# Seven products for the first pass's down projection, with its activations kept in DRAM

## The chip, the cores and the metric

The kernel runs on one core of one Trainium2 chip. The metric is the device time of one execution in microseconds. Three runs of the kernel before gave a median of 1057.07 us (1052.88 to 1057.88).

## What is computed

Attention of 4 batches x 12 heads x 448 tokens x 64, with a soft cap, is followed by two layers on the 1792 x 768 result (d_ff is 2048). The second layer has no part in the edit, but is in the kernel:

```python
scores = cap * tanh(q @ k.T / sqrt(64) / cap)
x = softmax(scores) @ v            # heads side by side: 1792 x 768
h = x @ moe_w_in                   # 768 x 2048
g = h - tanh(h)
x = g @ moe_w_out                  # 2048 x 768
h = x @ moe2_w_in
g = h * sigmoid(1.702 * h)
out = g @ moe2_w_out
```

The four weight matrices come as float64.

## The kernel before

**Tiling.** Activations lie transposed, 128 features on the partitions and tokens along the free axis. The tokens are worked through in two passes, the first of 768 and the second of 1024 (`TOKENS`). A matmul has 128 x 128 weights and takes half a pass, 384 or 512 columns. Each factor is split into a high part (rounded to fp32r) and a low part (the rest); a product is three matmuls: high x high, high x low, low x high. A split is one cast on ScalarE (`hi_act`, L81) and one subtraction on VectorE (`lo_dve`, L93).

**Stages.** After attention (to 187.8 us) come, in this order: **P1-up** (`gemm_in(0)`, first pass, 16 blocks f of 128 features, 36 matmuls each); **P1-down** (`gemm_out`, L927); **P2-up** (`gemm_in(0)` again, second pass); **P2-down** (`gemm_out_seven`, L979); **P2-gate** (`gemm_in_seven`, the second layer's up projection of the second pass); then `gemm_rows_seven`, and both stages of the second layer for the first pass. "Seven" means that a product of 2 x 2 blocks is done by seven half-size products instead of eight: each sums blocks of weights (made once, kept in DRAM as `s1` to `s4`, `t1` to `t4`) and blocks of activations (made just before use, in `right` and `left`), splits them, and adds the results. In P2-down each of the seven products has four steps; a step takes one weight block of 128 x 768 and issues 18 matmuls, and at each step `right` makes the next product's activations into a `ring` of eight split blocks. P1-down is the plain form: 2 halves x 8 steps x 36 matmuls, with g of all 16 blocks held split (`gh`, `gl`) in on-chip memory.

**Weights.** A block of float64 weights is loaded (`dbl_dma`, 768 KB), turned into float32 in three instructions (`conv_exp` and `conv_low` on ScalarE or VectorE, `conv_or` on VectorE, L219) and loaded again next to it. For w_in1 the split parts are kept in DRAM for the second pass (`kept`). w_out1 is converted and split for P1-down at the time of use, and its float32 blocks are written to DRAM (`single`), read back by `sums_a` during P2-up, summed, and stored. `sums_i` converts and sums moe2's w_in, `sums_b` its w_out. In the stages by seven products a block comes back by `fetch` into two or three buffers (`whole`, `spare`) and is split into `wh` and `wl`.

**Order.** Matmuls go in program order. Two blocks of weights are prepared ahead (`LEAD`). Side work (`sums_a`, `sums_i`, `sums_b`) is cut into pieces by `yield`; `ahead` and `beside` add `rate[0]` to an account at each call and take a piece for each whole unit. Each piece stands behind the last instruction of ScalarE and VectorE in the trace at that point, with lower priority. All engines and SP's queue, which issues nearly all transfers, take their instructions in order. In an up projection, `g_cubic` takes tanh from PSUM, and a later call (`late`) does the rest: three ScalarE passes and three of VectorE over a block.

```python
    def g_split(f, g):
        yield hi_act(gh[f], g)
        yield lo_dve(gl[f], g, gh[f])
```

## Time and profile before

| | |
|---|---|
| median of three runs | 1057.07 us |
| profiled execution | 1055.68 us |
| its span | 1053.9 us |
| TensorE busy | 1038.7 us, 99% of the span, 5483 matmuls recorded |
| weight loads busy | 857.8 us, 81% |
| VectorE busy | 819.6 us, 78%, 1097 instructions |
| ScalarE busy | 692.0 us, 66% |
| granted clock of TensorE | 1.00 in all stages |
| transfers | 218.17 MB, mean 207 GB/s |

Shares over the whole span mix stages with different limits. The table says that TensorE is the engine to look at; whether another engine limits it in a stage shows in the view of busy time by stage, in the chain that ended last, and in the waits. Matmuls overlap, so the cost of one is read from the start of the first to the start after the last, not from the duration of one.

### The profile page before, as it was taken

To read this page: it belongs to the slowest core of one execution; us is meant where nothing else is said; L and a number is where in the kernel's file an instruction comes from. 1 tells how busy PE (TensorE), PEld (TensorE's weight loads), DVE (VectorE), ACT (ScalarE), POOL (GpSimd) and SP (SyncE) were. 2 spreads that over 40 slices of the span, in tenths; PEclk is the share of its full clock that TensorE was granted. 3 is DMA by queue.
4 is the path that set the end of the run, shared out by engine and by line. 5 is a ranking of instruction groups with operands and counts; after the bars stand their busy time and mean duration, and the time that the engine had idled before them with its cause. 6 is when DMAs were issued, how large, how long until landed. Compare 5 with 4: busy or idle time off the path is not lost.

```text
span 1053.9 us, 15397 instructions
## 1 busy us (share of the span) xinstructions
PE 1038.7 (99%) x5483; PEld 857.8 (81%) x5483; DVE 819.6 (78%) x1097; ACT 692.0 (66%) x958; POOL 56.1 (5%) x56
## 2 busy tenths in 40 slices
PE   8999999999999999999999999999999999999998
PEld 3333333899999998888878888887899999999998
DVE  4799999899986517988899897685899974448973
ACT  6999898787854335556775757655755745557663
POOL 0123444100000000000000000000000000000000
PEclk9999999999999999999999999999999999999999
DMA  5777688765588958888673852898654554444443
GB/s 132 196 217 219 181 228 257 255 228 192 195 257 275 327 170 287 289 277 283 219 253 118 299 183 82 272 321 297 224 164 126 190 155 130 129 118 143 153 134 104
DMA packets 153749, 218.17 MB, mean 207 GB/s; under 512 B 58380, under 2 KB 101704, under 8 KB 153672
## 3 DMA queue, kind: packets, MB, share of 16 engines
q1 hardware_dynamic: 152376, 216.58, 64.9%
q8 instruction: 43, 0.70, 0.3%
q10 hardware_dynamic: 1296, 0.61, 0.2%
...
## 4 chain that ended last, share of the span: by engine, by line
PE 81%; DVE 11%; ACT 3%; DMA 3%; issue 2%; SPq 0%; DVEq 0%; ACTq 0%
PE ps_o L1194 19%; PE ps_h L912 19%; PE ps_h L1092 19%; PE ps_y L952 9%; PE ps_y L1005 5%; PE ps_pv L568 3%; PE ps_sc L526 3%; DVE gr L361 1%; DVE wl L93 1%; ACT t L545 1%; DVE rl L93 1%; DVE ts L557 1%; PE ps_r L582 1%; DVE ts L556 1%; PE ps_tl L536 1%
## 5 line engine op out<-in xcount | busy, mean ns | idle before, releaser
L81 ACT CAST rh<-gr 128x512 fp32r<-128x512 f32 (+1 forms) x179 | 103.6, 584 | 99.7 <-PE ps_o L1194 63.2
L912 PE MATMUL ps_h<-x,wh 128*128 128x384 f32 (+1 forms) x672 | 153.0, 358 | 0.0
L93 DVE TENSOR_TENSOR rl<-gr,rh 128x512 fp32r<-128x512 f32 (+1 forms) x179 | 113.8, 642 | 25.8 <-ACT rh L81 25.1
L1194 PE MATMUL ps_o<-wh,rl 128*128 128x384 f32 x392 | 131.1, 334 | 0.0
L1194 PE MATMUL ps_o<-wh,rh 128*128 128x384 f32 x392 | 131.1, 334 | 0.0
L1194 PE MATMUL ps_o<-wl,rh 128*128 128x384 f32 x392 | 131.1, 334 | 0.0
L912 PEld LDWEIGHTS ps_h<-x,wh 128*128 128x128 f32 x672 | 121.1, 188 | 12.0 <-issue 0.7
L93 DVE TENSOR_TENSOR wl<-whole,wh 128x768 fp32r<-128x768 f32 (+1 forms) x103 | 94.0, 912 | 13.7 <-ACT wh L81 12.8
L81 ACT CAST wh<-whole 128x768 fp32r<-128x768 f32 (+1 forms) x103 | 82.4, 800 | 24.7 <-PE ps_h L1092 10.6
L1092 PE MATMUL ps_h<-x,wh 128*128 128x384 f32 (+1 forms) x336 | 97.3, 359 | 0.0
L912 PE MATMUL ps_h<-x,wl 128*128 128x384 f32 (+1 forms) x384 | 88.1, 364 | 0.0
L545 ACT ACTIVATE t<-ps_sc,tsc 128x896 f32<-128x896 f32 x72 | 69.8, 1005 | 15.1 <-PE ps_sc L526 15.0
L912 PEld LDWEIGHTS ps_h<-x,wl 128*128 128x128 f32 x384 | 69.8, 188 | 9.7 <-issue 1.4
L1194 PEld LDWEIGHTS ps_o<-wl,rh 128*128 128x128 f32 x392 | 73.6, 188 | 0.0
L1194 PEld LDWEIGHTS ps_o<-wh,rh 128*128 128x128 f32 x392 | 73.6, 188 | 0.0
L1194 PEld LDWEIGHTS ps_o<-wh,rl 128*128 128x128 f32 x392 | 73.6, 188 | 0.0
L547 ACT ACTIVATE t<-t,cpos 128x896 f32<-128x896 f32 x72 | 72.4, 1042 | 0.4
L526 PE MATMUL ps_sc<-qk 64*128 64x448 f32 x288 | 68.3, 568 | 2.3 <-ACT t L545 1.5
L361 DVE TENSOR_TENSOR gr<-gr 128x512 f32<-128x512 f32 (+2 forms) x112 | 69.3, 645 | 0.6 <-DMA gr<-xa 0.4
L361 DVE TENSOR_TENSOR part<-ps_h,part 128x512 f32<-128x512 f32 (+1 forms) x48 | 29.8, 621 | 51.3 <-PE ps_h L1092 51.1
L1092 PE MATMUL ps_h<-x,wl 128*128 128x512 f32 (+1 forms) x192 | 69.6, 362 | 0.0
L219 DVE SCALAR_TENSOR_TENSOR wr<-wr,wd 128x768 uint32<-128x768 uint32 x48 | 46.0, 961 | 28.4 <-ACT wd L211 20.7
...
## 6 DMA issues: line engine op xcount, KB each, us to landing
...
```

Of the source, the lines that this page charges most:

```text
L81: pin(nc.scalar.copy(out=dst, in_=src))
L93: return pin(nc.vector.tensor_tensor(out=dst, in0=src, in1=hi.bitcast(F32), op=ALU.subtract))
L219: pin(nc.vector.scalar_tensor_tensor(out=u, in0=u, scalar=3, in1=dbls.pop(i)[:, :, 0], op0=ALU.logical_shift_left, op1=ALU.bitwise_or))
L361: nc.vector.tensor_tensor(out=out, in0=a, in1=b, op=kind)
L526: pin(nc.tensor.matmul(ps[:, j, :S], qk[a, kc], qk[a, :S], start=True, stop=True))
L545: pin(nc.scalar.activation(out=t, in_=ps[:, :, :S], func=AF.Tanh, scale=tsc))
L547: ins = pin(nc.scalar.activation(out=tt[g, c], in_=tt[g, c], func=AF.Exp, scale=cpos))
L912: pin(nc.tensor.matmul(ps, w[:, kk, :], x[kk][:, a], start=(m == 0), stop=(m == len(seq) - 1)))
L952: nc.tensor.matmul(bank[e][:, :a1 - a0], w[:, kk, c], x[2 * j + kk][:, a0:a1], start=(j == 0 and m == 0), stop=(j == KF // 2 - 1 and m == ...
L1005: nc.tensor.matmul(ps[e], w[:, kk, c], x, start=(name == head and k == 0 and m == 0), stop=(k == KH - 1 and m == 2), skip_group_check=True,)
L1092: nc.tensor.matmul(ps, w, x, start=(name == head and m == 0), stop=(m == len(seq) - 1), skip_group_check=True,)
L1194: nc.tensor.matmul(ps[n], x[:, t], w[:, kk, :], start=(first and k == 0 and m == 0), stop=(k == KH - 1 and m == 2), skip_group_check=True,)
```

## The change

The order of the stages becomes P1-up, P2-up, P1-down, P2-down, and P1-down is done by seven products (`gemm_out_first`): the first pass's g leaves for DRAM after P1-up (`ga`), and comes back in 16 loads of a quarter of a block row each (`load_quarter`) into the room that the second pass's x had. The second pass's x is loaded and scaled in P1-up instead of P1-down. The products' activation sums are made in `first_right`; those of the first product are split during P2-up. w_out1 is no longer split from the converted block: `sums_a` converts it in groups of four blocks during P2-up and sums these in place, and P1-down fetches float32 blocks and sums as P2-down does. `sums_i` starts after `sums_a` and runs on through P1-down (rate 0.5 in its last six steps) and P2-down (1.1 instead of 0.8); `sums_b` runs at 1.45 instead of 1.2. The third buffer for weights is taken for every third block by number.

```diff
+    ga = dr_p.tile([2 * KM + 4, P, TOKENS[0]], F32, name="ga")
...
-    order = early + [i for i in range(R0) if i not in early] + [R0 + n % 4 * KQ + n // 4 for n in range(KF)]
+    order = early + [i for i in range(A0) if i not in early]
+    order += [A0 + n * KQ + j for j in range(KQ) for n in (3, 2, 0, 1)] + list(range(I0, R0)) + [R0 + n % 4 * KQ + n // 4 for n in range(KF)]
...
-    limit = [I0]
+    gr, wd_slot = [], []
+
+    limit = [A0]
...
+        elif A0 <= i < I0:
+            raws[i] = group[(i - A0) // KQ]
...
+    SEVEN_1 = ("11", "12", "s4", "s3", "s2", "s1", "22")
...
+            whole[i] = third[0] if third and i % 3 == 0 else wr_p.tile([P, WC], F32, tag="wr", name="whole")
...
     def sums_a():
+        limit[0] = I0
+        for _ in range(3):
+            dbl_dma()
+        yield
         for j in range(KQ):
-            r = four_of_pairs()
-            for n, t in enumerate(r):
-                nc.sync.dma_start(out=t, in_=single[n * KQ + j])
-                if n % 2:
-                    yield
-            for m, t in first_sums(*r):
+            group_of_four()
+            for n in (3, 2, 0, 1):
+                i = A0 + n * KQ + j
+                convert(i)
+                raws.pop(i)
+                yield
+            for m, t in first_sums(*group):
                 nc.sync.dma_start(out=side_a[m][j], in_=t)
                 yield
         done.add("a")
 
-    def sums_i(first, end):
-        limit[0] = I0 + 2 * end if end < KH else NCH
-        for _ in range(2):
...
-    def g_split(f, g):
-        yield hi_act(gh[f], g)
-        yield lo_dve(gl[f], g, gh[f])
...
+            q = gr[f][:, :n] if now[0] else first_g[f]
...
+            if not now[0]:
+                nc.sync.dma_start(out=ga[f], in_=q)
...
+        if now[0] and f < KH // 2:
+            for k in (2 * f, 2 * f + 1):
+                late.append(lambda k=k: split([t[:, :FH] for t in ring[k]], first_g[k][:, :FH]))
...
+    def open_first_g():
+        p = x_pool("ga")
+        for name in ("21", "22", "12", "11"):
+            quarter[name] = [p.tile([P, 2, FH], F32, name=f"g{name}_{n}") for n in range(KQ)]
...
+    def load_quarter(name, n):
+        f = 2 * n + (KH if name[0] == "2" else 0)
+        a = slice(FH, FT) if name[1] == "2" else slice(0, FH)
+        nc.sync.dma_start(out=quarter[name][n], in_=ga[f:f + 2, :, a].rearrange("k p c -> p k c"))
...
+    def first_right(p, k):
+        g11, g12, g21, g22 = (g_of(name, k) for name in ("11", "12", "21", "22"))
+        if p > 2:
+            with tc.issue_after(behind[k].ins):
+                if p == 3:
+                    sub(g12, g22, g12)
+                elif p == 4:
+                    add(g11, g11, ALU.add, g12)
+                elif p == 5:
+                    sub(g22, g22, g11)
+                elif p == 6:
+                    sub(g21, g21, g11)
+        behind[k] = split([t[:, :FH] for t in ring[k]], {1: g21, 2: g22, 3: g12, 4: g11, 5: g22, 6: g21}[p])
...
+                    if m == LATE_AT and a0 and not now[0]:
+                        if f:
+                            if loaded:
+                                x_scale(*loaded.pop(0))
+                        for _ in range(1 if f else 3):
+                            if todo:
+                                loaded.append((*todo[0], *x_load(*todo.pop(0))))
...
-    def gemm_out():
...
+    def gemm_out_first():
+        LO, HI = slice(0, FH), slice(FH, FT)
+        loads = [(name, n) for name in ("21", "22", "12", "11") for n in range(4)]
+        p1 = u3 = None
+        u7 = [g_of("12", e) for e in range(3)]
+        u1 = [g_of("12", 3 + e) for e in range(3)]
+        of, head_of = {}, {"s2": "11", "s1": "11", "22": "s3"}
+        step = 0
+
+        def leave(e, a, x):
+            nc.sync.dma_start(out=xa[e][:, a], in_=x)
+
+        six = [one_bank("ps_y")[:, :FH] for _ in range(6)]
+        nc.vector.memset(six[0][:1, :1], 0.0)
+        of["11"], of["12"] = six[1:4], six[4:] + six[:1]
+        for p, name in enumerate(SEVEN_1):
+            head = head_of.get(name, name)
+            if head not in of:
+                spread = [ps_s.tile([P, 512], F32, tag="s", name="ps_y") for _ in range(2 if head == "s4" else 0)]
+                of[head] = [t[:, :FH] for t in spread + [one_bank("ps_y") for _ in range(3 - len(spread))]]
+            ps = of[head]
+            for j in range(KQ):
                 i, (wh, wl) = w_next()
-                for (a0, a1), bank in zip(SPANS[0], ps):
-                    for e in range(3):
-                        c = slice(e * P, (e + 1) * P)
-                        seq = [p for kk in range(2) for p in ((wh, gh, kk), (wh, gl, kk))]
-                        seq += [(wl, gh, kk) for kk in range(2)]
-                        for m, (w, x, kk) in enumerate(seq):
+                for _ in range(2 if step < 2 else 1):
+                    if loads:
+                        load_quarter(*loads.pop(0))
+                rate[0] = .5 if step >= 22 else 0.0
+                ahead(i)
+                for e in range(3):
+                    c = slice(e * P, (e + 1) * P)
+                    for kk in range(2):
+                        k = 2 * j + kk
+                        h, l = (t[:, :FH] for t in ring[k])
+                        for m, (w, x) in enumerate(((wh, h), (wh, l), (wl, h))):
                             nc.tensor.matmul(
-                                bank[e][:, :a1 - a0], w[:, kk, c], x[2 * j + kk][:, a0:a1],
-                                start=(j == 0 and m == 0), stop=(j == KF // 2 - 1 and m == len(seq) - 1),
+                                ps[e], w[:, kk, c], x,
+                                start=(name == head and k == 0 and m == 0), stop=(k == KH - 1 and m == 2), skip_group_check=True,
                             )
+                if 1 <= step <= KQ:
+                    for k in (2 * step - 2, 2 * step - 1):
+                        first_right(1, k)
+                if p:
+                    for k in (2 * j, 2 * j + 1):
+                        if p < 6:
+                            first_right(p + 1, k)
+                        else:
+                            right(0, k)
+                if step == 0:
+                    run_late()
+                step += 1
+            if p == 0:
+                p1 = [part_of(t) for t in ("far", "far", "v")]
+            elif p == 2:
+                u3 = [part_of(t) for t in ("q", "q", "t")]
+            with tc.high_priority(offset=AHEAD):
+                for e in range(3):
+                    if name in ("11", "s4", "s3", "s2"):
+                        nc.scalar.copy(out={"11": p1, "s4": u3, "s3": u7, "s2": u1}[name][e], in_=ps[e])
+                    elif name == "12":
+                        add(p1[e], ps[e], ALU.add, p1[e])
+                    elif name == "s1":
+                        add(u3[e], ps[e], ALU.add, u3[e])
+                        add(u7[e], ps[e], ALU.add, u7[e])
+                    else:
+                        add(u1[e], ps[e], ALU.add, u1[e])
+            for e in range(3):
+                if name == "12":
+                    leave(e, LO, p1[e])
+                elif name == "s1":
+                    leave(e, HI, u3[e])
+                    leave(3 + e, HI, u7[e])
+                elif name == "22":
+                    leave(3 + e, LO, u1[e])
...
-                rate[0] = .8 if 2 <= p * KQ + j < 5 * KQ else 0.0
+                rate[0] = 1.1 if 2 <= p * KQ + j < 5 * KQ else 0.0
...
-            rate[0] = 1.2 if j else 0.0
+            rate[0] = 1.45 if j else 0.0
...
     def moe():
         yield from gemm_in(0)
-        gemm_out()
+        run_late()
         to_pass(1)
-        plain[0] = True
         some.pop("stack").close()
-        open_plain()
-        side_p.append(end_of_x.enter_context(tc.tile_pool(name="side", bufs=2, side="right", reuse_waits="tile")))
+        open_second()
         open_wide()
         side.append(sums_a())
-        side.append(sums_i(EARLY_I, KH))
+        side.append(sums_i())
         rate[0] = 1.5
         yield from gemm_in(0)
         run_late()
@@ -1271,11 +1363,17 @@
         open_banks(False)
         open_temps()
         third[:] = spare
+        to_pass(0)
+        open_first_g()
+        gemm_out_first()
+        open_x_again()
+        to_pass(1)
         gemm_out_seven()
         third[:] = [gr[2 * KH - 1][:, :WC]]
         side.append(sums_b())
         gemm_in_seven()
         until("b")
+        again[0]()
         gemm_rows_seven()
```

**VectorE in P2-up.** Before (names: `pair` are four blocks of w_out1 read back from DRAM, `rl` the low part of a split block for the next stage, `g_far`, `g_t` and `gr` the four passes over a block of g):

```order
L812 SCALAR_TENSOR_TENSOR gr<-gr,g_t 128x1024
L813 COPY_PREDICATED gr<-g_m,g_far 128x1024
L361 TENSOR_TENSOR pair<-pair 128x768
L93 TENSOR_TENSOR rl_3991<-gr,rh_3990 128x512
L361 TENSOR_TENSOR pair<-pair 128x768 x2
L799 TENSOR_TENSOR g_far<-ps_h,g_t 128x1024
L361 TENSOR_TENSOR pair<-pair 128x768
```

And now (`group` and `spare` are the four blocks being converted, `wd` the loaded float64 block):

```order
L211 SCALAR_TENSOR_TENSOR group<-group,wd 128x768
L795 TENSOR_TENSOR g_far<-ps_h,g_t 128x1024
L804 TENSOR_TENSOR g_t<-g_v,g_t 128x1024
L805 SCALAR_TENSOR_TENSOR gr<-gr,g_t 128x1024
L806 COPY_PREDICATED gr<-g_m,g_far 128x1024
L353 TENSOR_TENSOR group<-group 128x768
L211 SCALAR_TENSOR_TENSOR group<-group,wd 128x768
L795 TENSOR_TENSOR g_far<-ps_h,g_t 128x1024
```

The sums stand on the converted blocks themselves, with the conversions' last instruction between them; the splits have moved to the first four blocks.

**VectorE at the end of P2-up.** Before, the next stage being P2-down (`wl<-whole` and `wl<-spare` are the low parts of its weight blocks, the last row being the fourth):

```order
L219 SCALAR_TENSOR_TENSOR wr<-wr,wd 128x768
L361 TENSOR_TENSOR gr<-gr 128x512
L93 TENSOR_TENSOR wl<-whole,wh 128x768
L799 TENSOR_TENSOR g_far<-ps_h,g_t 128x1024
L810 TENSOR_TENSOR g_t<-g_v,g_t 128x1024
L361 TENSOR_TENSOR wr<-wr 128x384
L812 SCALAR_TENSOR_TENSOR gr<-gr,g_t 128x1024
L361 TENSOR_TENSOR wr<-wr 128x384
L813 COPY_PREDICATED gr<-g_m,g_far 128x1024
L93 TENSOR_TENSOR rl_3983<-gr,rh_3982 128x512
L93 TENSOR_TENSOR wl<-spare,wh 128x768
```

And now, the next stage being P1-down:

```order
L806 COPY_PREDICATED gr<-g_m,g_far 128x1024
L89 TENSOR_TENSOR wl<-whole,wh 128x768
L795 TENSOR_TENSOR g_far<-ps_h,g_t 128x1024
L211 SCALAR_TENSOR_TENSOR wr<-wr,wd 128x768
L804 TENSOR_TENSOR g_t<-g_v,g_t 128x1024
L1012 MEMSET ps_y 1x1
L805 SCALAR_TENSOR_TENSOR gr<-gr,g_t 128x1024
L806 COPY_PREDICATED gr<-g_m,g_far 128x1024
L89 TENSOR_TENSOR rl_3078<-g_0_4195,rh_3077 128x384
L89 TENSOR_TENSOR wl<-whole,wh 128x768
```

The sums for the second product (`gr<-gr`) are gone here; the first splits of the second product (`rl`) read loaded blocks `g_0`, and the low part of the fourth weight block stands behind the first of them.

**VectorE in P1-down.** Before (x is the second pass's, `wl<-wr` the low part of a converted block):

```order
L93 TENSOR_TENSOR x<-x 128x512
L1249 TENSOR_TENSOR x<-x 128x512
L93 TENSOR_TENSOR wl<-wr,wh 128x768
L93 TENSOR_TENSOR x<-x 128x512
L213 TENSOR_SCALAR wd<-wd 128x768
L219 SCALAR_TENSOR_TENSOR wr<-wr,wd 128x768
L213 TENSOR_SCALAR wd<-wd 128x768
L93 TENSOR_TENSOR wl<-wr,wh 128x768
L219 SCALAR_TENSOR_TENSOR wr<-wr,wd 128x768
```

And now (`g_0` to `g_3` are loaded blocks of g):

```order
L353 TENSOR_TENSOR g_0_4199<-g_0_4199,g_0_4207 128x384
L89 TENSOR_TENSOR rl_3090<-g_3_4210,rh_3089 128x384
L89 TENSOR_TENSOR wl<-whole,wh 128x768
L89 TENSOR_TENSOR rl_3092<-g_3_4210,rh_3091 128x384
L353 TENSOR_TENSOR g_0_4199<-g_0_4199,g_0_4207 128x384
L353 TENSOR_TENSOR g_1_4200<-g_1_4200,g_1_4208 128x384 x2
L89 TENSOR_TENSOR rl_3078<-g_0_4199,rh_3077 128x384
L89 TENSOR_TENSOR wl<-spare,wh 128x768
L89 TENSOR_TENSOR rl_3080<-g_0_4199,rh_3079 128x384
```

Conversions and the scaling of x are gone; two sums and two splits of 384 columns and one low part of weights per step have come.

## Rows read from the trace of the kernel before

**Rows 1.** Busy time by stage: P1-up, P1-down, P2-up, P2-down, P2-gate.

```profile
core 0: us, PE busy (x) PEld busy (x) DVE busy (x) ACT busy (x) POOL busy (x), PEclk, DMA share, GB/s
187.80:290.60 102.80, 102.80 (x593) 100.36 (x592) 93.33 (x105) 83.08 (x106) 0.25 (x1) 1.00 0.64 216
290.60:390.50 99.90, 99.90 (x578) 99.90 (x578) 53.39 (x71) 40.34 (x59) 0.00 (x0) 1.00 0.81 262
390.50:522.40 131.90, 131.90 (x577) 108.11 (x576) 109.15 (x113) 80.98 (x86) 0.00 (x0) 1.00 0.82 274
522.40:640.20 117.80, 116.01 (x507) 94.28 (x506) 112.84 (x168) 78.01 (x122) 0.00 (x0) 1.00 0.61 199
640.20:758.10 117.90, 116.67 (x505) 94.10 (x504) 81.69 (x113) 73.97 (x114) 0.00 (x0) 1.00 0.76 253
```

**Rows 2.** Chain that ended last, by time: start us, us, what.

```profile
...
290.93 99.84 PE ps_y L952 x576
390.77 97.72 PE ps_h L912 x426
...
726.63 5.20 DMA whole<-s
...
962.69 87.39 PE ps_o L1194 x504
```

**Rows 3.** Matmuls of P1-down (L952) and of P2-down (L1005), by their lines.

```profile
...
L952 PE MATMUL ps_y<-gh,wh x192: 333/335/335, 290.8 to 389.9; 128*128 128x384 f32 x192
...
L1005 PE MATMUL ps_y<-rh,wl x168: 388/389/501, 523.2 to 640.1; 128*128 128x512 f32 x168
```

**Rows 4.** Waits from 520 to 642 us: us, times, longest us.

```profile
...
PEld ps_y L1005 <- DVE wl L93: 3.4, 5, 1.2
...
PE ps_y L1005 <- DVE wl L93: 1.2, 2, 0.8
```

**Rows 5.** VectorE's groups by form, whole span: busy us, mean ns, idle before.

```profile
...
L93 DVE TENSOR_TENSOR wl<-whole,wh 128x768 fp32r<-128x768 f32 x92 | 87.9, 956 | 13.7 <-ACT wh L81 12.8
L93 DVE TENSOR_TENSOR rl<-gr,rh 128x512 fp32r<-128x512 f32 x117 | 79.5, 688 | 9.1 <-ACT rh L81 8.5 <-PE ps_o L1194 0.3
L219 DVE SCALAR_TENSOR_TENSOR wr<-wr,wd 128x768 uint32<-128x768 uint32 x48 | 46.0, 961 | 28.4 <-ACT wd L211 20.7 <-ACT wr L204 7.7
L361 DVE TENSOR_TENSOR gr<-gr 128x512 f32<-128x512 f32 x64 | 42.2, 688 | 0.1
L93 DVE TENSOR_TENSOR rl<-gr,rh 128x384 fp32r<-128x384 f32 x62 | 34.3, 554 | 16.8 <-ACT rh L81 16.6
L361 DVE TENSOR_TENSOR wr<-wr 128x384 f32<-128x384 f32 x32 | 17.8, 557 | 6.8 <-DMA single<-wr 6.5
L93 DVE TENSOR_TENSOR gl<-g_q,gh 128x768 fp32r<-128x768 f32 x16 | 15.3, 953 | 0.0
L1249 DVE TENSOR_TENSOR x<-x 128x512 f32<-128x512 f32 x12 | 8.3, 690 | 3.0 <-DMA x<-wrow 2.9
```

**Rows 6.** VectorE in order of time, P2-down: start us, us, what.

```profile
...
534.71 0.70 DVE L93 TENSOR_TENSOR rl<-gr,rh 128x512 fp32r<-128x512 f32 x1
535.30 0.97 DVE L93 TENSOR_TENSOR wl<-spare,wh 128x768 fp32r<-128x768 f32 x1
536.17 0.71 DVE L93 TENSOR_TENSOR rl<-gr,rh 128x512 fp32r<-128x512 f32 x1
536.77 0.57 DVE L361 TENSOR_TENSOR wr<-wr 128x384 f32<-128x384 f32 x1
537.24 0.70 DVE L361 TENSOR_TENSOR gr<-gr 128x512 f32<-128x512 f32 x1
...
634.85 1.90 DVE L93 TENSOR_TENSOR rl<-gr,rh 128x512 fp32r<-128x512 f32 x3
```

**Rows 7.** VectorE's waits for converted weights, 406 to 645 us; their conversions' count.

```profile
...
DVE wr L219 <- ACT wd L211: 2.7, 2, 2.1
...
DVE wr L219 <- ACT wr L204: 2.4, 2, 1.2
...
DVE wr L361 <- DMA single<-wr: 2.0, 2, 1.5
...
L219 DVE SCALAR_TENSOR_TENSOR wr<-wr,wd x13: 949/955/961, 407.1 to 596.9; 128x768 uint32<-128x768 uint32 x13
```

**Rows 8.** Busy time within P2-gate, columns as in group 1.

```profile
...
680.00:700.00 20.00, 20.00 (x89) 16.38 (x88) 16.71 (x23) 13.27 (x21) 0.00 (x0) 1.00 0.90 319
700.00:720.00 20.00, 20.00 (x89) 16.42 (x88) 12.72 (x18) 9.88 (x16) 0.00 (x0) 1.00 0.94 312
```

179 lines of the change are left out of this document (80 added, 99 removed).

## Prediction

> **What bounds the kernel now.** I read the busy time by stage first, to see which engine fills each stage. TensorE fills all five stages from 187.8 to 758.1 us at a granted clock of 1.00 [rows 1], so a stage is worth what its matmuls cost, unless another engine fills it too. Three more numbers of that view matter: VectorE is busy 53.39 of 99.9 us in P1-down, 109.15 of 131.9 in P2-up and 112.84 of 117.8 in P2-down. VectorE is thus a second, almost equal bound where seven products are taken, and has room where the plain form is taken. Then the chain that ended last: through P1-down it is one piece of matmuls, 99.84 us for 576, or 0.1733 us each; through P2-up 97.72 us for 426, or 0.2294 us each [rows 2]. With that pitch the 504 matmuls of P2-down should take 115.6 us, and the stage lasts 117.8; P2-gate lasts 117.9. So P2-down holds 2.2 us of waiting and P2-gate 2.3. Last the waits: in P2-down TensorE's two rows wait for low parts of weights on VectorE, 3.4 and 1.2 us [rows 4]; in P2-gate the chain goes through one fetch of a weight block, 5.20 us [rows 2].
>
> **The change, part by part.** *P1-down by seven products.* 576 matmuls of 384 columns [rows 3] become 504 of 384 columns; P2-down already issues such a sequence (3 x 168, rows 3) and the 384-column products of the first pass's second layer run 504 in 87.39 us [rows 2], the same 0.1734 us. Removed from the path: 72 x 0.1733 = **12.5 us**. The order changes (P2-up now stands ahead of P1-down), but P1-up, P2-up and the rest keep their matmuls.
>
> *P1-up.* It loses 16 splits of g (0.953 us each on VectorE) and gains the 12 scalings (0.690) and 12 splits (about 0.688) that read the second pass's x [rows 5]: 15.3 us out, 16.5 in. The conversions of the first w_out blocks, which ran ahead into this stage, leave it. VectorE is busy 93.33 of 102.8 us here [rows 1] without TensorE waiting, so I cost this at nothing; the cover is that slack and three pairs of PSUM banks. Transfers grow by 16 stores of g (384 KB each, 6.3 MB) and 12 x loads (512 KB with the broadcast rows, 6.3 MB), and lose the early w_out reads (8 of 768 KB) and 5 stores of 384 KB: 216 GB/s x 102.8 us = 22.2 MB becomes about 27 MB, some 270 GB/s. P2-up runs at 274 GB/s today with no wait of TensorE [rows 1], so nothing again.
>
> *P2-up.* VectorE's list: the four passes over each g block and 16 sums of 768 columns stay; 16 conversions of w_out1 enter; 7 conversions of w_in2 become 4 and their 18 sums of 384 become 4; 7 sums of 512 leave; 8 splits of 512 become 384 wide. With the durations of rows 5: 13 x 0.961 - 14 x 0.557 - 7 x 0.688 - 8 x 0.134 = -1.2 us. The load is equal, so is the lateness I expect at the end; but 20 conversions wait here instead of 7. A conversion and its sums cost VectorE (2.7 + 2.4 + 2.0)/13 = 0.55 us of idle time between 406 and 645 us [rows 7]: 7 us more idle time, in a stage where VectorE idled 22 us [rows 1]. I let it be absorbed. Loads of 768 KB replace reads of sums of 384 KB: about 38 MB in 131.5 us, 290 GB/s.
>
> *The joint P2-up to P1-down.* This is where I expect the new wait. At today's joint (P2-up to P2-down) the low part of the fourth weight block starts at 535.30 us and takes 0.97 [rows 6], so it is there 13.9 us after the stage began at 522.4; a block of 18 matmuls lasts 4.13 us there, so it is needed after 12.4. Behind the change a block lasts 18 x 0.1733 = 3.12 us and the fourth is needed after 9.4. With the same lateness TensorE waits 4.5 us. It could be nothing, if the last g block is ready sooner, or 12 us, if the 7 us of idle time all arrive here. I take **+4.5**, the value from the nearest row. What waited at the beginning of P2-down (2.2) goes, since nothing is left over from an up projection there: **-2.2**.
>
> *Inside P1-down.* VectorE's list: 100 instructions of 384 columns (48 splits, 32 sums, 12 adds from PSUM, 8 sums of weights), 30 of 768 (28 low parts, 2 conversions), 8 of 512. What one costs is read from rows 6, where no wait stands between: 0.59 us from a 512 start to the next start, 0.87 for 768, 0.47 for 384, while the durations are 0.70, 0.97 and 0.57. So 100 x 0.47 + 30 x 0.87 + 8 x 0.60 = 77.9 us, in 87.3 us of matmuls. Cost: nothing, and 9 us to make up lateness. The 16 loads of g are issued from the moment the last matmul of P2-up frees x, and the first is needed at the second product, 12.5 us in; they stand on SP's queue ahead of the sixth weight block, needed after 15.6 us.
>
> *P2-down and the joint to P2-gate.* 10 conversions instead of 6, 6 more sums of 384 and 7 more of 512: by starts 4 x 0.87 + 6 x 0.47 + 7 x 0.60 = 10.5 us more, and 4 x 0.55 = 2.2 of idle time. But today VectorE reaches the second product's first split 12.3 us after this stage's start (534.71, rows 6); behind the change the backlog has fallen to P1-down and it can begin after the first block, some 8 us earlier. Today it comes to the splits for P2-gate at 634.85 [rows 6], 5.3 us ahead of the stage's end: 10.5 + 2.2 - 8 leaves it about even. I take **+1** between 0 and 6 (6 if most of the 8 us are not there).
>
> *P2-gate.* The rate of side work goes from 1.2 to 1.45 a block, so its transfers crowd: shares of 0.90 and 0.94 stand there already [rows 8]. On the other hand the third buffer for weights is now taken in strict turn. Between -2.3 (the wait goes) and +3 I take 0.
>
> **Sum.** -12.5 - 2.2 + 4.5 + 1 = -9.2. The profiled execution took 1055.68 us (span 1053.9): 1046.5. The median of the runs is 1.4 us above that execution, so **1048 us** for the median. The ends of the unknown costs: -12.5 - 2.2 - 2.3 = -17.0, or 1040; -12.5 - 2.2 + 12 + 6 + 3 = +6.3, or 1063.
>
> **Rivals.** *A, no new wait.* The last g block is ready as early as TensorE needs it and the fetches of P2-gate come in turn: -17.0, **1040 us**. For it: ring and weights are filled well ahead in the list; against it: all waits that rows 4 show are of just this kind. *B, transfers come in bursts in P2-up.* The w_out1 blocks are converted four at a time, into two buffers of 768 KB; ScalarE takes its work in order, so a conversion whose load is late holds back tanh behind it. Where transfers crowd so, P2-gate loses 2.3 us at a share of 0.94 [rows 1, 8]. Four such groups: 4 x 2.3 = 9.2 on top of the forecast, **1057 us**, no change. For it: 290 GB/s is more than P2-up has now; against it: P2-up at 0.82 shows no wait of TensorE. *C, VectorE is the bound.* If its instructions do not overlap, P1-down and P2-down need the full durations: 100 x 0.554 + 30 x 0.956 + 8 x 0.688 = 89.6, and 119.9 us for today's list of P2-down (34 instructions of 768 columns, 115 of 512, 15 of 384) with 4 x 0.961 + 6 x 0.557 + 7 x 0.688 = 12.0 on top, 221.5 us against 202.9 of matmuls; before it was 119.9 against 115.6. The excess grows by 14.3 us, and the 13 + 4 more conversions idle 17 x 0.55 = 9.4: -12.5 + 23.7 = +11.2, **1068 us**, slower. It decides once VectorE's work in the two stages passes 202.9 us. Against it are the starts in rows 6, which lie 0.1 us closer than the durations; for it, that VectorE was 96% busy in P2-down. The Trainium skill states the rule behind C (VectorE: DVE Perf Modes, section "The DRAIN you can't avoid"): the next operation does not start until the pipe of the one before is empty; the same section adds that one that isn't held starts earlier, and the rows side with that. That the change doesn't do what it says is excluded by its instruction order: 504 matmuls of 384 columns stand in P1-down.
>
> **How the numbers follow.** Forecast 0.60 (1043 to 1052), A 0.12, B 0.16, C 0.12. About 0.5%, or 5.3 us, is what a measurement of this kernel can tell from no change, so the bounds are 1051.8 and 1062.4. Faster: A and nearly all of the forecast, 0.71. Same: B and a rest of the forecast, 0.17. Slower: C, 0.12. The range 1040 to 1058 takes in the forecast, A's middle and B, and leaves out C and a half of A: about 0.8.
>
> **What would show it.** P1-down as 504 matmuls at 0.173 us, some 88 to 92 us long with its waits, all in its first product and put down to low parts of weights; P2-down at 115.6 to 117 us with VectorE over 95% busy; P2-up at 132. Wrong would be: P2-up over 135 us with waits on DMA of w_out (B), P1-down and P2-down with waits spread over all products and VectorE never idle (C), or no wait at the joint (A).

## The result, and the profile after

The changed kernel takes **1068.4 us** (median) beside 1056.8 for the kernel before on the same chip: a ratio of 1.0111, 95% interval 1.0076 to 1.0146. It is slower, where 1048 us was forecast. One of its four runs took 1455.2 us at a granted clock of 0.655; it is left out of the ratio, and the median of the other three is 1067.9 us. Its profiled execution took 1068.94 us with a span of 1067.1, 13.2 more than before.

Busy time by stage of the changed kernel, with the columns of [rows 1]; the order is P1-up, P2-up, P1-down, P2-down, P2-gate, second-layer rows of the second pass:

```profile
188.40:294.10 105.70, 105.26 (x594) 102.36 (x593) 92.75 (x108) 73.95 (x96) 2.03 (x2) 1.00 0.88 297
294.10:424.80 130.70, 130.70 (x579) 108.24 (x578) 112.23 (x111) 101.61 (x112) 0.00 (x0) 1.00 0.88 306
424.80:524.60 99.80, 93.37 (x505) 91.78 (x504) 85.81 (x143) 61.70 (x107) 0.00 (x0) 0.97 0.74 250
524.60:642.20 117.60, 117.60 (x505) 94.62 (x505) 110.76 (x168) 77.51 (x122) 0.00 (x0) 1.00 0.67 213
642.20:769.10 126.90, 120.87 (x505) 96.10 (x504) 91.68 (x128) 73.29 (x114) 0.00 (x0) 0.97 0.80 273
769.10:887.80 118.70, 118.70 (x673) 118.69 (x672) 98.79 (x156) 67.46 (x116) 0.00 (x0) 1.00 0.45 135
```

P1-down has its 504 matmuls and still lasts 99.8 us, as long as the 576 before [rows 1]. P2-gate lasts 8.9 us more. In both, TensorE idles for some 6 us, and the granted clock is 0.97. P2-down, where VectorE's busy share is highest, has no wait of TensorE. Counted from a stage's first matmul to the next stage's, the 13.2 us come from these stages:

| stage | forecast, us | measured, us |
|---|---|---|
| attention and the two up projections | 0 | +0.5 and +1.4 |
| P1-down with the joint before it | -12.5 + 4.5 | 0.0 |
| P2-down | -2.2 + 1 | 0.0 |
| P2-gate | 0 | +8.9 |
| the three last stages | 0 | +2.4 |

**P1-down.** Its waits: us in all, times, longest:

```profile
ACT wd L203 <- DMA wd<-in_moe_w_in_dram: 6.1, 2, 3.3
PE ps_y L1033 <- ACT wh L77: 5.0, 2, 3.9
ACT wr L196 <- DMA s<-wr: 4.9, 3, 2.0
```

ScalarE in order of time there (start us, us):

```profile
431.79 1.13 ACT L803 ACTIVATE g_m<-g_v,cub_u 128x1024 bf16<-128x1024 f32 x1
436.26 0.88 ACT L203 ACTIVATE wd<-wd 128x768 uint32<-128x768 uint32 x1 [3.34 <-DMA wd<-in_moe_w_in_dram]
437.04 0.50 ACT L77 CAST rh<-g 128x384 fp32r<-128x384 f32 x1
437.44 0.83 ACT L77 CAST wh<-whole 128x768 fp32r<-128x768 f32 x1
```

and TensorE, with the windows around its wait below:

```profile
434.13 0.33 PE L1033 MATMUL ps_y<-rh,wl 128*128 128x384 f32 x1
438.32 0.44 PE L1033 MATMUL ps_y<-rh,wh 128*128 128x384 f32 x1 [3.85 <-ACT wh L77]
440.08 0.52 PE L1033 MATMUL ps_y<-rl,wh 128*128 128x384 f32 x1
443.25 0.34 PE L1033 MATMUL ps_y<-rh,wh 128*128 128x384 f32 x1
```

```profile
434.00:439.00 5.00, 1.08 (x5) 0.45 (x3) 3.39 (x4) 2.74 (x5) 0.00 (x0) 1.00 1.03 356
439.00:443.00 4.00, 3.68 (x12) 3.69 (x13) 4.00 (x8) 3.18 (x7) 0.00 (x0) 0.57 1.00 341
454.00:474.00 20.00, 17.80 (x90) 16.84 (x89) 16.38 (x29) 10.49 (x20) 0.00 (x0) 0.91 0.97 350
```

A conversion of the second layer's input matrix (L203, side work of `sums_i`) stands on ScalarE for 3.34 us, waiting for its load. The transfers are at a share of 1.00 to 1.03 here, with the first five of the 16 quarter loads of g beside it. Behind it, in order, stands the cast of the fourth weight block (437.44), for which TensorE waits 3.85 us. Then the granted clock falls, and a matmul takes 0.52 us in place of 0.34: 1.2 instead of 2.4 GHz, after a wait and not before it. From 454 us on TensorE waits again, three times (0.65, 1.17 and 0.37 us), and the clock falls behind the last of these; the longest is for a cast that itself waits 1.43 us for its weight block (`wh<-spare`, 464.22), with no side conversion just ahead of it. By their starts, 15 matmuls stand in the 9 us from 434 and 88 in the 20 from 454; they should take 2.6 and 15.5 us at 0.1765, so 10.8 us are lost: 6.4 us of waits, some 3.5 us at the lower clock (0.43 x 4 and 0.09 x 20), and the rest in starting again.

**P2-gate.** The last stores of `sums_i` leave SP's queue at 605 us in the kernel before and at 650 in the changed one, 8 us into P2-gate:

```profile
605.07 1.50 SPq L409 DMA_DIRECT2D s<-wr  x2
```

```profile
649.90 2.46 SPq L411 DMA_DIRECT2D s<-wr  x2
```

The chain that ended last goes, in P2-gate, through the store of a group of weight sums, where [rows 2] had one fetch; ScalarE beside it:

```profile
735.96 6.91 DMA t<-group
...
769.27 118.72 PE ps_o L1288 x672
887.99 88.03 PE ps_h L1186 x504
976.01 87.38 PE ps_o L1288 x504
```

```profile
742.97 0.89 ACT L196 ACTIVATE group<-wd 128x768 f32<-128x768 f32 x1 [3.95 <-DMA t<-group]
...
746.27 0.82 ACT L77 CAST wh<-whole 128x768 fp32r<-128x768 f32 x1
```

The next group's conversion writes the buffer that this store reads; it waits 3.95 us on ScalarE, and a weight's cast behind it. For that cast TensorE waits 4.6 us, 105 us into the stage, and the clock falls at the end of the wait:

```profile
PE ps_h L1186 <- ACT wh L77: 4.6, 1, 4.6
740.00:769.00 29.00, 24.43 (x93) 18.88 (x92) 20.74 (x28) 18.64 (x30) 0.00 (x0) 0.88 0.68 238
```

The clock costs some 3.5 us of these 29 (0.12 x 29). Together that is 8.1 of the 8.9 us. Before this place TensorE waits only 1.5 us in the whole stage, and not at all in its first 34 us, where the tail of `sums_i` runs. In the kernel before the same conversion waits 0.85 us, and TensorE not at all behind it:

```profile
738.76 0.91 ACT L204 ACTIVATE group<-wd 128x768 f32<-128x768 f32 x1 [0.85 <-DMA t<-group]
```

**The pitch.** The 672 matmuls of the chain's 118.72 us take 0.1767 us each, and the 504 at the end 0.1734. Groups of matmuls of the changed kernel by form (busy us, mean ns):

```profile
L1288 PE MATMUL ps_o<-wh,rl 128*128 128x384 f32 x392 | 132.6, 338 | 0.0
L977 PE MATMUL ps_h<-x,wh 128*128 128x384 f32 x384 | 73.2, 339 | 0.4 <-DMA wh<-kept 0.4
L1099 PE MATMUL ps_y<-rh,wl 128*128 128x512 f32 x168 | 67.0, 399 | 0.0
```

The kernel before had 334 to 335 ns for 384 columns and, up to P2-down, 390 to 393 for 512, but not with one tile, which only its own rows by form show:

```profile
L912 PE MATMUL ps_h<-x,wh 128*128 128x512 f32 x288 | 81.1, 390 | 0.0
L912 PE MATMUL ps_h<-x_end,wh 128*128 128x512 f32 x96 | 38.2, 397 | 0.0
L1092 PE MATMUL ps_h<-x,wh 128*128 128x384 f32 x192 | 48.8, 335 | 0.0
L1092 PE MATMUL ps_h<-x_end,wh 128*128 128x384 f32 x48 | 12.4, 339 | 0.0
```

`x_end` was the only tile of TensorE at the right end of on-chip memory. The change puts the first pass's x and the ring there. The right end lies 32 bytes short of a multiple of 64: in the built program x_end starts at byte 217056 of a partition, x now at 192480 and the ring at 196576 (224 past a multiple of 256), while all operands at the left, the weights among them, start 128 past one.

### The profile page after: what moved, and what is told of

It reads as the page before. It is cut to its first block, busy times and chain, and to the rows that moved or that the text cites. A ratio compares the mean times of both kernels' runs of the same rounds, so it can differ in the third digit from the quotient of the medians.

```text
span 1067.1 us, 15533 instructions
## 1 busy us (share of the span) xinstructions
PE 1042.0 (98%) x5411; PEld 856.6 (80%) x5411; DVE 859.0 (80%) x1179; ACT 724.1 (68%) x1025; POOL 55.9 (5%) x56
## 5 line engine op out<-in xcount | busy, mean ns | idle before, releaser
L77 ACT CAST rh<-gr 128x512 fp32r<-128x512 f32 (+1 forms) x187 | 107.7, 580 | 105.0 <-PE ps_o L1288 72.5
L89 DVE TENSOR_TENSOR rl<-gr,rh 128x512 fp32r<-128x512 f32 (+1 forms) x187 | 118.2, 637 | 31.4 <-ACT rh L77 30.2
L1186 PE MATMUL ps_h<-xb,wh 128*128 128x384 f32 (+1 forms) x432 | 122.9, 365 | 4.6 <-ACT wh L77 4.6
L89 DVE TENSOR_TENSOR wl<-whole,wh 128x768 fp32r<-128x768 f32 (+1 forms) x121 | 110.6, 914 | 17.1 <-ACT wh L77 15.8
L77 ACT CAST wh<-whole 128x768 fp32r<-128x768 f32 (+1 forms) x121 | 96.7, 800 | 17.7 <-PE ps_h L1186 11.9
L977 PE MATMUL ps_h<-xb,wh 128*128 128x512 f32 x384 | 92.3, 389 | 0.0
L1186 PEld LDWEIGHTS ps_h<-xb,wh 128*128 128x128 f32 x432 | 80.3, 190 | 13.4 <-ACT wh L77 5.0
L977 PEld LDWEIGHTS ps_h<-xb,wh 128*128 128x128 f32 x384 | 72.1, 188 | 14.9
L1186 PE MATMUL ps_h<-xb,wl 128*128 128x384 f32 (+1 forms) x216 | 78.7, 364 | 0.0
L977 PE MATMUL ps_h<-x,wh 128*128 128x384 f32 x384 | 73.2, 339 | 0.4 <-DMA wh<-kept 0.4
L977 PEld LDWEIGHTS ps_h<-x,wh 128*128 128x128 f32 x384 | 68.0, 188 | 1.4 <-DVE gr L806 0.7
```

The lines of the kernel that those rows point to most:

```text
L77: pin(nc.scalar.copy(out=dst, in_=src))
L89: return pin(nc.vector.tensor_tensor(out=dst, in0=src, in1=hi.bitcast(F32), op=ALU.subtract))
L977: pin(nc.tensor.matmul(ps, w[:, kk, :], x[kk][:, a], start=(m == 0), stop=(m == len(seq) - 1)))
L1186: nc.tensor.matmul(ps, w, x, start=(name == head and m == 0), stop=(m == len(seq) - 1), skip_group_check=True,)
```

## The experiments

All times are medians in us beside the kernel before on the same chip; stages are of the profiled execution, from a stage's first matmul to the next one's. That execution can lie off the median: 4.2 us below it in a_edge, 3.7 above in d_early, 6.7 above in d_early7.

| run | us | ratio (95%) | P1-down | P2-down | P2-gate | rows, 2nd pass |
|---|---|---|---|---|---|---|
| before | 1057 | 1 | 99.8 | 117.6 | 118.0 | 116.5 |
| after | 1068.4 | 1.0111 (1.0076 to 1.0146) | 99.8 | 117.6 | 126.9 | 118.7 |
| a_edge | 1068.9 | 1.0099 (1.0064 to 1.0135) | 97.3 | 115.4 | 127.3 | 118.7 |
| a_edge24 | 1062.8 | 1.0043 (1.0026 to 1.0061) | 96.6 | 114.3 | 129.9 | 116.5 |
| b_shift | 1059.1 | 1.0022 (1.0005 to 1.0039) | 99.9 | 115.3 | 118.7 | 116.5 |
| a_up11 | 1085.2 | 1.0255 (1.0231 to 1.0278) | 89.0 | 117.6 | 122.7 | 150.9 |
| a_pause | 1073.9 | one run | 89.0 | 117.6 | 123.0 | 138.1 |
| a_spread | 1059.0 | one run | 89.8 | 117.6 | 127.2 | 118.7 |
| a_gate12 | 1069.4 | 1.0107 (1.0080 to 1.0135) | 97.1 | 117.6 | 127.8 | 118.2 |
| a_down14 | 1068.4 | one run | 98.1 | 117.6 | 128.0 | 118.7 |
| b_gate145 | 1055.5 | one run | 99.8 | 116.5 | 118.6 | 116.5 |
| a_all | 1057.3 | 1.0011 (0.9999 to 1.0023) | 88.0 | 115.4 | 129.2 | 118.7 |
| c_late12 | 1058.4 | 1.0008 (0.9986 to 1.0029) | 87.4 | 115.4 | 129.0 | 119.0 |
| c_late | 1053.4 | 0.9955 (0.9939 to 0.9972) | 88.0 | 114.5 | 131.2 | 116.5 |
| c_late12e | 1056.9 | 0.9992 (0.9972 to 1.0013) | 87.5 | 114.3 | 133.7 | 118.4 |
| d_notail | 1043.7 | one run | 89.2 | 114.3 | 119.3 | 116.5 |
| d_early | 1055.5 | 0.9981 (0.9965 to 0.9997) | 88.5 | 123.5 | 126.0 | 116.5 |
| d_early7 | 1053.7 | 0.9972 (0.9951 to 0.9993) | 88.5 | 121.3 | 125.7 | 116.5 |
| e_early12 | 1053.5 | 0.9957 (0.9939 to 0.9974) | 87.6 | 117.6 | 126.5 | 118.4 |
| e_third | 1052.3 | 0.9958 (0.9939 to 0.9976) | 89.4 | 119.6 | 122.4 | 116.5 |

### The place of the operands

On the changed kernel, a_edge (a_edge24 has `[P, 24]`):

```diff
+    pool("edge", 1, side="right").tile([P, 8], F32, name="edge")
     right_side = ExitStack()
```

On the kernel before, b_shift:

```diff
+    pool("edge", 1).tile([P, 8], F32, name="edge")
     big = pool("big", 1)
+    pool("edge2", 1).tile([P, 8], F32, name="edge2")
```

*a_edge:* 

> The changed kernel with one unused column of 32 bytes a partition at the end of on-chip memory, so that the first pass's x, the ring and the rest of the right side start at a multiple of 64 bytes, where they now start at 32 past one (the program's addresses). Theory (the place of an operand against 64 bytes sets TensorE's pitch): the 384-column matmuls that read x or the ring fall from 338 to 340 ns to the 334 to 335 of the other tiles, the 512-column ones of P2-down from 392 to 399 to about 390. About 3 ns for each of 576 (P1-up), 504 (P1-down) and 1176 (second-layer rows of both passes) and 4 for each of 504 (P2-down): some 8 to 9 us, so about 1060 us. Rival 1 (far end of the memory, whatever the offset): durations unchanged, 1068 us. Rival 2 (more transfers beside TensorE slow its reads): unchanged, 1068 us.

*b_shift:* 

> The kernel before with 32 unused bytes a partition ahead of its x tile and 32 behind it, so that x alone, at the low end of the memory, starts 32 bytes past a multiple of 64, and all other tiles stay at multiples. Theory (offset against 64 bytes): the matmuls that read x rise from 335 to 339 ns (384 columns) and from 390 to 392 towards 397 (512 columns), as those that read x_end already show: P1-up +1.8, P2-up some +1.5 to +2.5, P2-gate and P1-gate under +1 each, about 1061 us. Rivals (far end of the memory, or the transfers): durations unchanged, 1056.8 us.

*a_edge24:* 

> The changed kernel with 96 unused bytes at the end of memory and nothing else, so that x and the ring start 128 bytes past a multiple of 256 as in the kernel before. Theory (the place alone): P1-up and P2-up together 236.4 to 234.7 us, P2-down 117.6 to 114.5, rows of the second pass 118.7 to 116.5, P1-gate 88.0 to 87.4, P1-down about 1.6 less with its waits kept, P2-gate within 3 of 126.9: 1068 to about 1059 us, between 1056 and 1063. Rival (those stages were shorter through the other mends of that run): 1064 us or more, with P2-down at 116 or above.

In a_edge, x and the ring stand at a multiple of 64 bytes (192 past one of 256): x falls to 336 ns, P2-down to 115.4 us, but the rows stay at 118.7 and those of the first pass grow by 1.7. So the theory of 64 bytes holds for x and P2-down and fails for the rows. The total did not move, though its runs scatter (1064.7 to 1072.1) and its profiled execution has a span of 1062.8. In b_shift x stands at 160 past a multiple of 256, at the low end. Its two paddings also move every tile behind x by 64 bytes, to 192 past one. Its x, and its rows beside those of a_edge (last line):

```profile
L914 PE MATMUL ps_h<-x,wh 128*128 128x512 f32 x288 | 82.5, 395 | 0.0
L914 PE MATMUL ps_h<-x,wh 128*128 128x384 f32 x384 | 71.9, 336 | 0.0
L1196 PE MATMUL ps_o<-wh,rl 128*128 128x384 f32 x392 | 131.0, 334 | 0.0
L1289 PE MATMUL ps_o<-wh,rl 128*128 128x384 f32 x392 | 132.5, 338 | 0.0
```

So 390 becomes 395 without the far end and without more transfers. But the tiles at 192 lose nothing: P1-down keeps 334 ns, P2-down 389 to 390 and the rows 334, though a ring at 192 cost the rows 4 ns in a_edge, where the weights had stayed at 128. With 96 bytes all operands stand at 128 past a multiple of 256, still at the far end, and all is as before:

```profile
L1289 PE MATMUL ps_o<-wh,rl 128*128 128x384 f32 x392 | 130.9, 334 | 0.0
L978 PE MATMUL ps_h<-x,wh 128*128 128x384 f32 x384 | 72.1, 335 | 0.6 <-DMA wh<-kept 0.6
L1100 PE MATMUL ps_y<-rh,wl 128*128 128x512 f32 x168 | 65.4, 389 | 0.0
```

Both rivals fall. The 96 bytes alone bring 0.7% by the two ratios, about 7 us, less than the 9 expected, since P2-gate gives 3 back. In the rows the ring is the stationary operand, so the place counts there too. In the up projections of the first layer, both down projections and the rows, all five programs fit one rule: what counts is not an operand's own offset but whether both operands of a matmul stand at the same one (128 and 128, or 192 and 192). The second layer's up projections do not keep to it (394 ns for the 512-column matmuls of `rl` in P2-gate of b_shift, with both at 192), so the rule is not shown; that the place is the cause is.

### The joint to P1-down

The side rate of P2-up in a_up11; the pause in `gemm_in` of a_pause; a_spread is a_pause with the rate of P1-down:

```diff
-        rate[0] = 1.5
+        rate[0] = 1.1
...
-            if now[0] and f == KF - 1:
+            if now[0] and f >= KF - 3:
                 rate[0] = 0.0
...
-                rate[0] = .5 if step >= 22 else 0.0
+                rate[0] = .5 if step >= 10 else 0.0
```

*a_up11:* 

> The changed kernel with the side rate of P2-up at 1.1, from 1.5, so that the sums of the second input matrix (12 of 33 steps now, their loads and stores with them) begin behind the joint. Theory (conversions of that matrix, waiting on ScalarE for loads that stand among the 16 quarter loads of g, hold up the casts behind them): the 3.9 us wait for wh at 438 goes, P1-down falls from 99.8 to 90 to 94 us; 12 steps more in P2-gate may give 2 to 4 us back there; total 1060 to 1065 us. Rival 1 (the quarter loads and the stream's own weights alone fill the transfers): P1-down stays within 2 us of 99.8. Rival 2 (VectorE is the bound of the joint): P1-down falls by under 3 us, with waits for DVE wl in place of those for ACT wh.

*a_pause:* 

> The changed kernel with the sums of the second input matrix paused from the last three blocks of P2-up on, so that what has been started there is done before the joint. Theory (its conversions wait on ScalarE for loads that stand beside the quarter loads of g, and hold up the casts behind them): the 3.9 us wait for wh at 438 goes, P1-down falls from 99.8 to 89 to 92 us; six steps go to later stages, so P2-gate stays at 125 to 131; total 1058 to 1064 us. Rival 1 (the quarter loads alone fill the transfers): P1-down stays above 96. Rival 2 (the mere amount of the sums in P1-down, wherever they start): P1-down 94 to 97.

*a_spread:* 

> The pause of the run before, and in P1-down the side rate of 0.5 from the 10th of its 28 steps on instead of from the 22nd, which gives the six steps back there. Theory: P1-down 89 to 92 us although it now holds six steps more than with the pause alone, as nothing of them stands at the joint; P2-gate no better than 124 to 127; total 1056 to 1062 us. Rival (the amount of sums in P1-down is what costs, VectorE being at 86 us of 99.8 now): P1-down 94 us or more, with waits for DVE.

P1-down in a_pause and in a_spread:

```profile
425.10:514.20 89.10, 89.10 (x506) 89.08 (x505) 80.80 (x135) 58.63 (x102) 0.00 (x0) 1.00 0.68 222
```

```profile
424.60:514.50 89.90, 89.36 (x506) 89.02 (x505) 84.67 (x142) 62.33 (x107) 0.00 (x0) 1.00 0.80 272
```

The wait is gone in all three, at the same quarter loads, so it is the side work that stood at the joint; that six steps more of it in a_spread cost only 0.8 us speaks against the rivals on amount and on VectorE. What a_up11 and a_pause put off came due before the rows, where what is left of `sums_b` runs at one go (`until`; 19.5 us of waiting in a_pause); of a_up11:

```profile
PE ps_o L1288 <- ACT wh L77: 26.1, 2, 25.3
```

Only 2 to 4 us of that were expected. In a_up11 the last 18 matmuls of P2-gate stand among the rows and are counted there.

### P2-gate

a_gate12 (b_gate145 is the reverse, on the kernel before), and a_down14:

```diff
-            rate[0] = 1.45 if j else 0.0
+            rate[0] = 1.2 if j else 0.0
...
-                rate[0] = 1.1 if 2 <= p * KQ + j < 5 * KQ else 0.0
+                rate[0] = 1.4 if 2 <= p * KQ + j < 5 * KQ else 0.0
```

*a_gate12:* 

> The changed kernel with the side rate of P2-gate back at 1.2, from 1.45. Theory (at 1.45 the next group of conversions stands in ScalarE's order before the stores of the last group have landed, and the weights' casts stand behind it): P2-gate falls from 126.9 to about 118 us, the wait for the cast of wh at 747 goes, total about 1060 us. Rival (the stage is held by transfers at 0.8 to 0.97 share, brought by the sums whenever they run): P2-gate stays above 124, total 1066 to 1068 us.

*a_down14:* 

> The changed kernel with the side rate of P2-down at 1.4, from 1.1, so that the sums of the second input matrix end in P2-down; now their last stores leave at 650 us, 8 us into P2-gate, where the kernel before had them out at 605. Theory (P2-gate pays for that tail; the rate of its own sums is not the cause, as the run at 1.2 showed): P2-gate falls from 126.9 to 117 to 120 us, P2-down grows by 0 to 4 (VectorE is at 110.8 of its 117.6 us now), total 1060 to 1066 us. Rival (P2-gate is held by the transfers of the first column of sums itself): P2-gate stays above 124, total 1068 us or above.

*b_gate145:* 

> The kernel before with P2-gate's side rate at 1.45, from 1.2, and nothing else. Theory (the rate crowds P2-gate by itself): P2-gate rises from 118.0 to 122 to 127 us, total 1061 to 1066 us. Rival (the rate is free where the earlier sums end by 605 us, as here): P2-gate 117 to 120, total 1055 to 1058 us.

The rate alone is not the cause: 1.2 leaves P2-gate at 127.8, and 1.45 costs the kernel before 0.6 us. The waits do change with it: at 1.2 TensorE waits 2.0 us instead of 4.6 for the cast, and 4.5 us instead of 0.9 for VectorE's sums of partial results (`part`). a_down14 still has the last stores of `sums_i` at 643 us, 3 us into the stage, so it does not test the tail. Three runs do; all have 96 unused bytes, the pause, and P2-down at 1.4. d_notail has 0.5 from step 10 in P1-down and the loop of `sums_i` cut (with its entries in the load order and in the stream); d_early has 0.8 from step 8, d_early7 0.7 from step 10:

```diff
-        for j in range(KH):
+        for j in range(KH - 3):
...
-                rate[0] = .5 if step >= 22 else 0.0
+                rate[0] = .8 if step >= 8 else 0.0
```

*d_notail:* 

> The kernel with 96 unused bytes, the pause, 0.5 from the 10th step and P2-down at 1.4, with the last three of the eight pairs of the second input matrix's sums left out (neither loaded, converted nor summed; their places in the stream take the fifth pair's weights, so the output is not the reference's). P2-gate's weight stream and its own sums are the same in number. Theory A (the tail): P2-gate 117 to 120 us. Rival B (something of P2-gate's own): 126 or above.

*d_early:* 

> The kernel with 96 unused bytes, the pause and P2-down at 1.4, but P1-down's side rate 0.8 from its 8th step instead of 0.5 from its 10th (16 steps there, 7 more). Theory A (P2-gate pays for the tail of the sums of the second input matrix, whose last stores left at 635 us, 10 us into it; in the kernel before they left 36 us ahead of it): the last stores leave by about 605 us, P2-gate falls from 131.2 to 118 to 122 us, P1-down may grow by 0 to 3, total 1041 to 1046 us. Rival B (P2-gate is slow for something of its own in the changed kernel): P2-gate stays at 126 or above, total 1051 us or more. Rival C (VectorE is then the bound of P1-down): P1-down grows by 5 or more.

*d_early7:* 

> As the kernel with 0.8 from the 8th step, with 0.7 from the 10th (13 steps in P1-down). Theory A: last stores some 6 us later than there, P2-gate 119 to 125 us, total 1043 to 1049 us; rivals as there.

P2-gate of d_notail; P2-down and P2-gate of d_early; TensorE's longest wait in P2-gate of d_notail and of d_early:

```profile
627.50:746.80 119.30, 115.66 (x505) 94.21 (x505) 85.59 (x117) 74.41 (x114) 0.00 (x0) 1.00 0.79 264
```

```profile
512.90:636.40 123.50, 120.00 (x506) 95.68 (x505) 116.41 (x182) 77.96 (x123) 0.00 (x0) 0.97 0.70 229
636.40:762.30 125.90, 119.82 (x505) 97.24 (x504) 87.22 (x119) 74.02 (x114) 0.00 (x0) 0.96 0.76 254
```

```profile
PE ps_h L1187 <- ACT wh L77: 2.5, 1, 2.5
PE ps_h L1187 <- ACT wh L77: 4.0, 1, 4.0
```

With three of eight pairs of sums left out, P2-gate is 119.3. With them done earlier, P2-down pays 7 to 9 us (VectorE 116.41 of 123.5, TensorE waiting for low parts of the ring), and P2-gate is only at 126, though the last stores leave at 617 us, 19 ahead of it. So the tail explains a part (131.2 to 126 from c_late to d_early): c_late has 4.3 us of waits in the first 15 us of P2-gate, d_early none. What is left is the wait shown above. Some 100 us into the stage ScalarE stands for the store of a group 3.95 us in the changed kernel, 3.68 in c_late, 3.25 in d_early and 1.77 in d_notail, and TensorE behind it 4.6, 4.4, 4.0 and 2.5 us; only in d_notail the clock stays at 1.00. An earlier end of `sums_i` does not remove it. Nor is a late end of it that dear by itself: in a_pause its last stores leave 48 us into P2-gate, the group that is waited for comes only after the stage, and the stage takes 123.0. Two of the differences to the kernel before were tried on it, the rate and the turn of the third buffer (`fetch`, e_third):

```diff
-            whole[i] = third[0] if third and i % 3 == 0 else wr_p.tile([P, WC], F32, tag="wr", name="whole")
+            n_raw[0] += 1
+            whole[i] = third[0] if third and n_raw[0] % 3 == 0 else wr_p.tile([P, WC], F32, tag="wr", name="whole")
```

e_third is otherwise d_early7. By this count two live blocks can share the third buffer, so some weights are another block's; instructions and transfers stay the same in number. e_early12 has d_early7's P1-down, P2-down at 1.1 to the end of its sixth product, and P2-gate at 1.2.

*e_early12:* 

> 96 unused bytes, the pause, 0.7 from P1-down's 10th step, P2-down at 1.1 (to the end of its 6th product), P2-gate at 1.2. Theory (two things hold P2-gate: the tail of the earlier sums at its beginning, and, from about 80 us in, its own sums at 1.45, whose conversions stand on ScalarE before the stores of the last group have landed): with both relieved P2-gate takes 118 to 121 us and P2-down 115 to 119, total 1044 to 1049 us. Rival (the late waits are not the rate's): P2-gate stays at 124 or above with waits from 80 us in, total 1050 or above.

*e_third:* 

> 96 unused bytes, the pause, 0.7 from P1-down's 10th step, P2-down and P2-gate at 1.4 and 1.45, and the third buffer for weights taken by the count of the kernel before (fetches and conversions together) instead of in strict turn. Theory (strict turn makes a weight block wait for one certain buffer, so that its fetch comes late in P2-gate): the waits from 80 us in go, P2-gate 118 to 121 us, total 1047 to 1051 us. Rival (the rate, or the order of the stores of the sums): P2-gate as without this edit, 125 to 126 us, total 1053 to 1059 us.

The rate again leaves the stage as long (126.5). In e_third ScalarE waits only 0.3 us for the store of a group, TensorE at that place 0.9 us instead of 4.8 (and 2.9 us, 81 us in, behind the cast of a block that is fetched into the third buffer), the clock stays at 1.00, and P2-gate takes 122.4 instead of 125.7. This points at the turn of the third buffer, but does not show it: the blocks are not the right ones, it is one profile each, d_early7's is 6.7 us above its median, and the two ratios are not told apart. Why the store is waited for so much longer than in the kernel before stays open.

### All mends together

*a_all* (32 bytes, pause, 0.5 from step 10, P2-down at 1.1 to its sixth product): 

> All three mends in one: the 32 unused bytes at the end of memory, the pause at the joint with 0.5 from the 10th step of P1-down, and the rate of 1.1 of P2-down kept up to the end of its 6th product (4 blocks longer, 4 steps more). Theory: 99.8 to 89 in P1-down, 117.6 to 116 in P2-down, P2-up and P1-up 2 less, P2-gate 126.9 to 118 to 122: 1068 - 11 - 2 - 2 - 6 = 1047 us, between 1042 and 1053. Rival (each stage's saving is lost to the next, since the same steps must run somewhere and transfers or VectorE are full in each): 1058 us or above.

*c_late12* (32 bytes, pause, 0.5 from step 10, P2-down 1.4, P2-gate 1.2): 

> The three mends (32 unused bytes at the end of memory, pause at the joint with 0.5 from P1-down's 10th step) with P2-down's side rate at 1.4 instead of the longer stretch, and P2-gate's at 1.2. Theory (P2-gate pays for the tail of the earlier sums and, that gone, for its own sums at 1.45): P2-gate falls from 129.2 to 118 to 122 us, total 1044 to 1050 us. Rival (P2-gate's transfers are full whatever the rate): P2-gate 126 or above, 1054 us or above.

*c_late* (96 bytes, P2-gate at 1.45, else the same): 

> The same with P2-gate's side rate left at 1.45, and 96 unused bytes instead of 32, so that x and the ring start 128 bytes past a multiple of 256, as all moving operands of the kernel before do. Theory on the rate: P2-gate 125 to 129 us (the rate alone costs 5 to 8). Rival (only the tail costs): 118 to 121. Theory on the place (TensorE's pitch goes by the operands' offset within 256 bytes): the second-layer rows of the second pass fall from 118.7 to 116.5 us and those of the first from 89 to 87.4, P1-up's matmuls from 336 to 335 ns. Rival (far end of memory): rows stay at 118.7.

*c_late12e* (a_all with 96 bytes, P2-gate 1.2): 

> 96 unused bytes, the pause, P1-down from its 10th step, P2-down's 1.1 kept up to the end of its 6th product, and P2-gate's side rate at 1.2. Theory: P2-gate 118 to 123, rows of the second pass 116.5 to 118.7 after what the place is worth; total 1042 to 1050 us. Rival (transfers in P2-gate): 126 or above there and 1053 us or above in all.

In all four P2-gate stays at 129 to 134 us, where 118 to 123 was expected (125 to 129 in c_late), and with it the totals of the other three miss theirs. c_late takes 1053.4 us, 0.45% less than the kernel before, and e_early12 as much: the two fastest versions that keep the result; d_early7 and d_early lie 0.3 and 0.2% below the kernel before. In c_late the up projections (first row, both) take what they took before, and P1-down is 88.0; P2-gate (last row), 13 us longer than before, is what keeps it from 1040:

```profile
187.90:422.60 234.70, 233.78 (x1170) 208.62 (x1169) 202.91 (x217) 174.92 (x207) 0.58 (x1) 1.00 0.89 304
422.60:510.60 88.00, 87.66 (x505) 87.32 (x504) 81.67 (x138) 61.26 (x107) 0.00 (x0) 1.00 0.82 274
625.20:756.40 131.20, 120.29 (x506) 95.78 (x505) 97.65 (x137) 78.32 (x123) 0.00 (x0) 0.97 0.79 267
```

## Why the prediction was wrong

*Right:* the 12.5 us of 72 matmuls are there, 11.8 and 12.5 of them, once nothing is in the way (88.0 us in c_late, 87.4 in c_late12). P1-up and P2-up carry the stores, loads and conversions, at 297 and 306 GB/s where 270 and 290 were estimated (26.5 MB in 102.8 us is 258, not 270), and TensorE waits for them 0.4 us in all. P2-down runs without waits, with VectorE busy for 110.76 of its 117.6 us.

*The step that failed first is the joint.* It said: the fourth weight block comes late, 4.5 us, through VectorE's low part. The block and the size of that one wait were right (3.85 + 0.38 us at the fourth block), the engine was not: it was ScalarE, behind a side conversion whose load stood among the quarter loads. I had placed those loads on SP's queue and asked only when g is needed, not what they make late; and "the lateness I expect at the end" was read from a joint that had no such loads. The term was also too small: later waits, for a late weight block and for VectorE, and two falls of the clock make 10.8 us of 4.5. The clock's part was in no term. The Trainium skill says that the clock has two states, 1.2 and 2.4 GHz, and that idling leads to the lower (TensorE: Matmul & The Clock Gate, "What's actually happening"); the trace agrees (0.52 against 0.34 us a matmul).

*The second is P2-gate, taken at 0 between -2.3 and +3; it cost 8.9.* I looked at the rate and at the share of the transfers, and counted the strict turn of the third buffer as a gain. The runs show one wait that was in no term: ScalarE's conversion of a group behind the store of the group before it (3.95 us), TensorE behind ScalarE (4.6 us), and the lower clock after it (some 3.5 us). The side work also ends later, `sums_i` at 650 us instead of 605, since the plain P1-down, with VectorE busy for 53.39 of 99.9 us, is gone; I followed that lateness to P2-down's splits ("+1" between 0 and 6) and stopped there. But it is not what costs the 8.9 us: a_pause ends it later still and takes 123.0, d_early ends it ahead of the stage and has the wait. Its cause stays open; e_third points at the turn of the third buffer.

*The third is the pitch.* "P2-up and the rest keep their matmuls" was priced as the same time. The place of x and the ring made 384 columns 0.1765 us for 0.1733: 1.7 us in the up projections (beside c_late), 1.6 in P1-down, some 3 in P2-down and 2.2 in the rows. The row of x_end stood in the profile before. It also went into P2-up's 0.2294 us, which the prediction took for P2-down: c_late does P2-down in 114.5 us, under the 115.6 worked out from it, so the 2.2 us of waiting were more, and the slower pitch hid that they went.

*The rivals.* C named 1068 us, the time that came, by a mechanism that did not: P2-down has no wait for VectorE, and a_spread puts more on it in P1-down for 0.8 us. That the time came out as C's is chance. In P2-down TensorE waits for VectorE only where the runs put more side work around it, as in d_early, with 14 instructions more there (2.2 us). B's place was wrong (P2-up has no wait) and its mechanism right, a stage later: a conversion whose load is late holds back what stands behind it on ScalarE. A falls.
